# Row maxima of an attention sweep: float16 parts made by GpSimd, turned in four quadrants, copied by ScalarE and sent on-chip into the query stacks

## The chip, the core and the metric

The kernel runs on one core of a Trainium2 chip. A core has a matrix engine (TensorE, "PE" in the profile, its weight loads "PEld"), a vector engine (VectorE, "DVE"), an activation engine (ScalarE, "ACT"), a general engine (GpSimd, "POOL") and a queue engine that here issues all transfers (SyncE, "SP"). Each works through its own instructions in order; semaphores hold an instruction until what it needs is there. TensorE writes into PSUM, eight banks of 128 x 512 float32; the other data is in SBUF.

The metric is the device time of one execution in microseconds (us). The kernel before takes 1451.92 us, the median of 3 runs (1451.56 to 1452.12).

## What is computed

One transformer layer with parallel branches, on 2048 tokens of width 512, 32 heads of 16:

```python
xn = _layernorm(x, axis=-1)
qkv = (xn @ wqkv) ...                                   # 32 heads, head width 16
scores = einsum("bhqd,bhkd->bhqk", q, k) * (Dh ** -0.5)
p = softmax(scores, axis=-1)
o = einsum("bhqk,bhkd->bhqd", p, v) ... @ wo
h = gelu(xn @ w1 + b1)                                  # width 1792
return x + o + (h @ w2 + b2)
```

The softmax takes the maximum of each row of scores off before the exponential. That maximum, for each head and each query, is what the change is about.

## The kernel before

**Two passes over the scores.** The 32 heads are taken in 8 groups of four, the 2048 queries in 4 blocks of 512; a *block* t of the sweep is one group with one query block, so there are 32. Each block has 16 *units*. In unit u TensorE makes four kinds of products:

- **S**: scores of 128 queries against 512 keys, one product for each of the four heads (in the profile `pS<-kst,qst`). VectorE reduces each to one maximum for each query (`mt<-pS`, line 366): four reductions of 128 x 512 in each unit. This is the first pass, and only its maxima are kept.
- **E**: 19 units later (`LEAD`), the same scores again, turned over: 128 keys against 512 queries (`pT<-qst,kst`). ScalarE takes the exponential (`pe<-pT`, line 414).
- **V**: one or two units after that, the products of the exponentials with the values, in float32 (`pV<-pe,vv`), summed over the block's 16 units in one bank.
- **D**: dense products that fill the rest (projections, the two layers of the MLP, the output projection; `pD`), three or four for each half unit, as the table entries `FAST`, `MEAN` and `SLOW` say.

A unit has two halves. In the second one, which the change touches, TensorE's program reads E (head 2), S (head 3), S (head 2), E (head 3), then V, then D. All these products use 64 of the array's 128 rows and are cut into four column groups of 32, so that one product of the upper and one of the lower row half run beside each other; in the order of the program an E of one half stands beside an S of the other.

**Banks.** S products take turns in banks 0 to 2, E products in 3 to 5, D has bank 6, V bank 7. A product waits until its bank's last reader is done: S for the reduction three S products earlier, E for the exponential three E products earlier.

**The maxima.** The Q and K *stacks* (`qst`, `kst`) hold the operands of S and E: each head has 64 rows, of which 48 hold float16 parts of q or k. Rows 62 and 63 hold, in the K stack, the constant 1024, and in the Q stack, minus the query's maximum over 1024, as the sum of two float16 numbers. So the E product already has the maximum taken off; the S product leaves these two rows out. How the maxima come into the rows, for each block, is what changes:

1. at the end of the block's unit 15 (`s_end`), VectorE reduces the block's 64 maxima for each partition to 16 and negates them (`mneg<-mt`, line 382);
2. in the next unit (unit 0 of the next block's S pass), after the first half's products, TensorE turns them over by two float32 products with an identity (`ident,mneg`, line 390; the profile shows two passes for each), into a T or an S bank: S where a dense group has just begun;
3. VectorE reads the result twice and makes the float16 part and its rest (`mhl`, lines 393 and 394);
4. SyncE sends both to a scratch tensor in HBM with two transfers (`m_d<-mhl`, line 397), waits until they are there, and brings them into the stacks' rows with four (`qst<-m_d`, line 348).

The first E product of the block stands at the start of unit 3, that is 2 1/2 units after step 2. VectorE's next work behind step 1 are the four S reductions of unit 0; step 3 stands between its second and third.

**Order of the work.** Outside the first 90 us, nothing is planned at run time or by a scheduler: the program is written unit by unit (`unit`), each engine runs it in that order, and queues (`later`, `pooled`, `run_lane`) only decide in which unit an instruction is written. GpSimd's work is given out at the end of each unit with a budget of `POOL_NS` = 2500 ns. The first part is laid out by a list planner (`Plan`), with an estimated duration for each step; it holds the maxima of block 0.

Of the kernel before, what the change touches and what calls it, by code (L numbers as in the profile page):

```python
# [18 lines left out]
P = 128  # L19
# [15 lines left out]
POOL_NS = 2500  # L35
TAIL = 5
# [11 lines left out]
MROW = 1024.0  # L48
MROWS = struct.unpack("f", struct.pack("ee", MROW, MROW))[0]
# [5 lines left out]
def layer_kernel(ctx: ExitStack, tc: tile.TileContext, x, wqkv, wo, w1, b1, w2, b2, out):  # L55
# [19 lines left out]
    m_d = dram.tile([NG * NQB, 16, 2, P], F16, name="m_d")  # L75
# [21 lines left out]
    mnegs = [const.tile([P, 32], F32, name=f"mneg{i}") for i in range(2)]  # L97
    for m in mnegs:
        nc.gpsimd.memset(m, 0.0)
# [244 lines left out]
    def m_rows(t, h):  # L344
        g, qb = divmod(t, NQB)
        p, a = divmod(h, 2)
        dst = qst[g % 2][qb][64 * a + 62:64 * a + 64, p].rearrange("r (t q) -> r t q", q=P)
        nc.sync.dma_start(dst, m_d[t, 4 * h:4 * h + 4].rearrange("t r q -> r t q"))

    def s_mm(u, n, s):  # L350
# [7 lines left out]
        tiled(None, s, qs[qb][r, p, qt * P:(qt + 1) * P], ks[kb][r, p, :], True, True)  # L358
# [16 lines left out]
    def s_end(u):  # L375
# [4 lines left out]
        g, qb = divmod(t, NQB)  # L380
        mneg = mnegs[t % 2]
        nc.vector.tensor_reduce(mneg[:, :16], mt_of[t].rearrange("p h t k -> p (h t) k"), axis=AX.X, op=ALU.max, negate=True)
        given("dve", 220)

        def store():
# [3 lines left out]
            for a in range(2):  # L389
                nc.tensor.matmul(pt[32 * a:32 * a + 32, :64], mneg[64 * a:64 * a + 64, :],  # L390
                                 ident[64 * a:64 * a + 64, 64 * a:64 * a + 64], start=True, stop=True)
            mhl = work.tile([64, 2, 64], F16, name="mhl", bufs=2)
            nc.vector.tensor_scalar_mul(mhl[:, 0], pt[:64, :64], 1.0 / MROW)
            nc.vector.scalar_tensor_tensor(mhl[:, 1], pt[:64, :64], 1.0 / MROW, mhl[:, 0], op0=ALU.mult, op1=ALU.subtract)
            given("dve", 300)
# [96 lines left out]
    def last_one(osb):  # L492

        idle(3)
        on = work.tile([P, 4, 4, DH], F32, name="on")
# [1022 lines left out]
```

## Time and profile before

| | |
|---|---|
| median of 3 runs | 1451.92 us |
| the profiled execution | 1450.86 us, its span 1449.1 us |
| granted TensorE clock | 0.996 |
| busy: PE, DVE, ACT, POOL | 1432.0, 1353.8, 1255.9, 663.8 us |
| first and last `mneg` reduction of the sweep (31 of them) | 130.6 and 1384.7 us |

The span runs from the first to the last instruction. A matmul's end is modelled, so TensorE's busy time says less than when each product starts. A view of waits puts an engine's idle time down to what ended it; where a row says "issue", nothing that the profile shows ended it.

### The profile page before, as it was taken

The page shows a single profiled execution, that of the slowest core. Times are in us where ns is not written, and L with a number is a line of the kernel's source. Part 1 is how long each engine was busy: PE and PEld are TensorE (multiplying, and loading weights), DVE is VectorE, ACT ScalarE, POOL GpSimd, SP SyncE. Part 2 cuts the span into 40 slices and gives each one's busy share as a digit, 9 for nine tenths or more (in the row PEclk, how much of TensorE's full clock was granted, in tenths as well). Part 3 has the DMA queues.
Part 4 walks back from the last instruction along what each step waited for, and adds up shares of the span by engine and source line. Part 5 has one row for each costly group of instructions (what it writes and reads, how often), then busy time and mean ns, then how long its engine had stood idle before and what let it go on. Part 6 is the DMA issues. An engine that isn't in the chain of part 4 may idle for free.

```text
span 1449.1 us, 88687 instructions
## 1 busy us (share of the span) xinstructions
PE 1432.0 (99%) x40184; PEld 964.6 (67%) x40184; DVE 1353.8 (93%) x2304; ACT 1255.9 (87%) x2367; POOL 663.8 (46%) x673
## 2 busy tenths in 40 slices
PE   8999999999999999999999999999999999999998
PEld 4447767776666767667677766676766767666565
DVE  7989999999999999999999999999999999999933
ACT  5868888888999888899988899998889999888885
POOL 3201857664878401388831138882115787121100
PEclk9999999999999999999999999999999999999999
DMA  7731565455224210221112111121112110111423
GB/s 218 226 122 40 163 202 182 150 181 153 86 64 131 67 34 27 62 70 42 45 44 89 30 37 46 55 74 45 44 39 85 48 38 23 56 55 47 137 65 119
DMA packets 112627, 124.86 MB, mean 86 GB/s; under 512 B 22908, under 2 KB 84220, under 8 KB 112248
## 3 DMA queue, kind: packets, MB, share of 16 engines
q1 hardware_dynamic: 112248, 119.18, 26.8%
q8 instruction: 314, 5.14, 1.5%
q14 instruction: 65, 0.53, 0.1%
HBM read 81.66 MB, written 37.34 MB: 82 GB/s over the span
## 4 chain that ended last, share of the span: by engine, by line
PE 87%; DVE 8%; DMA 2%; ACT 1%; issue 1%; SPq 0%; DVEq 0%; ACTq 0%
PE pD L169 26%; PE pV L169 25%; PE pT L169 17%; PE pS L169 16%; DVE mt L366 7%; PE pT L1015 2%; DMA wq<-in_A_wqkv_dram 1%; PE pD L1015 1%; DMA m_d<-mhl 0%; ACT xs L968 0%; DVE xt L998 0%; ACT pe L414 0%; DMA qst<-m_d 0%; DVE ac L1393 0%; ACT wqk_h L904 0%
## 5 line engine op out<-in xcount | busy, mean ns | idle before, releaser
L366 DVE TENSOR_REDUCE mt<-pS 128x1 f32<-128x512 f32 x2029 | 1277.4, 682 | 34.8 <-PE pS L169 7.8
L414 ACT ACTIVATE pe<-pT 128x512 f32<-128x512 f32 x2048 | 1106.9, 599 | 150.2 <-PE pT L169 65.0
L169 PE MATMUL pV<-pe,vv 64*32 64x512 f32 x8192 | 1087.8, 591 | 0.3 <-issue 0.2
L169 PE MATMUL pT<-qst,kst 64*32 64x512 f16 x8192 | 710.4, 378 | 1.9 <-issue 1.2
L169 PE MATMUL pS<-kst,qst 62*32 62x512 f16 x8116 | 627.0, 378 | 2.6 <-DVE mt L366 2.0
L169 PEld LDWEIGHTS <-qst 62*32 62x32 f16 x8192 | 309.3, 90 | 196.7 <-issue 50.9
L169 PE MATMUL pD<-xb,wc 64*32 64x512 f16 x5376 | 363.9, 375 | 0.0
L169 PE MATMUL pD<-w_s,g 64*32 64x512 f16 x5376 | 361.8, 375 | 0.0
L169 PEld LDWEIGHTS <-kst 64*32 64x32 f16 x8192 | 280.5, 91 | 96.0 <-issue 24.2
L169 PEld LDWEIGHTS pV<-pe,vv 64*32 64x32 f32 x8192 | 245.3, 105 | 13.6 <-PE pV L169 4.2
L169 PEld LDWEIGHTS <-wc 64*32 64x32 f16 x5376 | 160.7, 91 | 44.5 <-issue 0.4
L169 PEld LDWEIGHTS <-g 64*32 64x32 f16 x5376 | 163.5, 91 | 39.2 <-issue 0.5
L169 PE MATMUL pD<-xt,wqk_h 64*32 64x512 f16 x2400 | 159.3, 376 | 0.7 <-issue 0.7
L1360 POOL TENSOR_TENSOR xa<-xa,yt 128x512 f32<-128x512 f32 x16 | 20.5, 1281 | 222.8 <-ACT yt L1358 222.8
L471 POOL TENSOR_TENSOR osb<-osb,rb 128x512 f32<-128x512 f32 x31 | 39.9, 1286 | 159.2 <-DMA rb<-den_d 132.8
L1312 POOL TENSOR_TENSOR t<-hh 128x512 f32<-128x512 f32 x56 | 58.2, 1040 | 77.0 <-ACT hh L1335 75.9
L169 PEld LDWEIGHTS <-wqk_h 64*32 64x32 f16 x2400 | 74.0, 92 | 19.9 <-issue 2.0
L1314 POOL TENSOR_TENSOR t<-t,hh 128x512 f32<-128x512 f32 x56 | 71.8, 1282 | 4.7
L1307 POOL TENSOR_TENSOR t<-t,hh 128x512 f32<-128x512 f32 x56 | 71.7, 1280 | 4.7
L1309 POOL TENSOR_TENSOR g<-t,g 128x512 f16<-128x512 f32 x56 | 65.2, 1164 | 4.7
L1306 POOL TENSOR_SCALAR t<-t,gs 128x512 f32<-128x512 f32 x56 | 38.8, 694 | 54.8 <-ACT t L1301 54.8
L169 PE MATMUL pD<-wo_s,oc 64*32 64x512 f16 x816 | 54.7, 376 | 0.0
(165 smaller groups left out, 895.1 us busy)
## 6 DMA issues: line engine op xcount, KB each, us to landing
wc<-w_d SPq DMA_DIRECT2D x56, 256.0 KB
qk_d<-stg SPq DMA_DIRECT2D x32, 256.0 KB
rb<-den_d SPq DMA_DIRECT2D x124, 64.0 KB
wch<-in_B_w_dram SPq DMA_DIRECT2D x14, 512.0 KB
wch<-in_B_w_dram SPq DMA_DIRECT2D x28, 256.0 KB
w_d<-wsp SPq DMA_DIRECT2D x28, 256.0 KB
kst<-qk_d SPq DMA_DIRECT2D x64, 96.0 KB
qst<-qk_d SPq DMA_DIRECT2D x64, 96.0 KB
```

The source lines that it names most:

```text
L169: p = nc.tensor.matmul(*args, **kw)
L366: nc.vector.reduce_max(mt_of[t][:, n, qt, kb:kb + 1], s, axis=AX.X)
L414: nc.scalar.activation(pe, st, AF.Exp, scale=scale_of[g // 2])
L471: pooled((1280, lambda: nc.gpsimd.tensor_tensor(osb, osb, rb, op=ALU.mult)), (620, lambda: nc.gpsimd.tensor_scalar(ot[:, 0], osb, 1.0, 0.0 ...
L1015: nc.tensor.matmul(tl[key], lhs, rhs, start=c + n == 0, stop=(c, n) == (NC - 1, 2))
L1306: pooled((690, lambda: nc.gpsimd.tensor_scalar(t1, t1, 1.0, gs[:, 1:2], op0=ALU.add, op1=ALU.mult)), (1280, lambda: nc.gpsimd.tensor_tenso ...
L1307: (1280, lambda: nc.gpsimd.tensor_tensor(t1, t1, hh, op=ALU.mult)),
L1309: (1160, lambda: nc.gpsimd.tensor_tensor(g[:, 1, f, :], t1, g[:, 0, f, :], op=ALU.subtract)),
L1312: pooled((1040, lambda: nc.gpsimd.tensor_tensor(t1, hh, hh, op=ALU.mult)), (620, lambda: nc.gpsimd.tensor_scalar(t1, t1, 1.0, 1.0 / GELU_A ...
L1314: (1280, lambda: nc.gpsimd.tensor_tensor(t1, t1, hh, op=ALU.mult)),
L1360: add = lambda: nc.gpsimd.tensor_tensor(xa, xa, yt, op=ALU.add)
```

## The change

After the change the steps for each block are these:

1. VectorE reduces to 16 maxima, without the sign (`mx<-mt`).
2. GpSimd divides by 1024 and makes the float16 part and its rest, three instructions of 128 x 16 elements, in the tile `mparts` (lines 363 to 365 of the changed kernel).
3. TensorE turns them with a negated float16 identity: 16 products of 64 rows, 32 columns, 64 moving columns (`m_turn`, line 373), each in one of four quadrants of 64 x 32 of the array, four times. They stand in the second half of unit 0, behind its second S product and ahead of its last E.
4. ScalarE copies 128 x 256 elements to float16 (`m_copy`, line 378).
5. SyncE issues four transfers from SBUF to SBUF, one for each head, straight into the stacks' rows (line 354). Nothing goes to HBM.

For the rows of a head to come out in one piece, the S products take their queries in another order: a tile of 128 queries is now two runs of 64 that lie 256 apart (`s_mm`). GpSimd's budget depends on the unit: 800 ns at the end of unit 14, 3100 ns at the end of units 15, 0 and 1 (`POOL_AT`), 2500 ns elsewhere, which makes 40,100 ns for each block in place of 40,000. Block 0 takes the same steps in the planner's part.

```diff
-    mnegs = [const.tile([P, 32], F32, name=f"mneg{i}") for i in range(2)]
+    nident = const.tile([P, P // 2], F16, name="nident")
+    for a in range(2):
+        nc.gpsimd.tensor_scalar(nident[64 * a:64 * a + 64], ident[64 * a:64 * a + 64, 64 * a:64 * a + 64], -1.0, 0.0,
+                                op0=ALU.mult, op1=ALU.add)
+    mparts = [const.tile([P, 64], F16, name=f"mparts{i}") for i in range(2)]
...
-        room[0] = min(room[0], 0) + POOL_NS
+        room[0] = min(room[0], 0) + (POOL_AT.get(pos[0] % 16, POOL_NS) if pos[0] < NU else POOL_NS)
...
+    def m_rows(t, turned, p, a):
         g, qb = divmod(t, NQB)
+        row = 64 * a + 62
+        nc.sync.dma_start(qst[g % 2][qb][row:row + 2, p, :], turned[2 * p + a:P:32])
+
+    def m_parts(t):
+        mx = work.tile([P, 4, 4], F32, name="mx", bufs=1)
+        parts = mparts[t % 2]
+        hi, lo = (parts[:, 16 * j:16 * j + 16].rearrange("p (t n) -> p n t", n=4) for j in range(2))
+        flat = mx.rearrange("p n t -> p (n t)")
+        return (lambda: nc.vector.tensor_reduce(flat, mt_of[t].rearrange("p h t k -> p (h t) k"), axis=AX.X, op=ALU.max),
+                lambda: nc.gpsimd.tensor_scalar(flat, flat, 1.0 / MROW, 0.0, op0=ALU.mult, op1=ALU.add),
+                lambda: nc.gpsimd.tensor_scalar(hi, mx, 1.0, 0.0, op0=ALU.mult, op1=ALU.add),
+                lambda: nc.gpsimd.tensor_tensor(lo, mx, hi, op=ALU.subtract)), parts
+
+    def m_turn(pt, parts):
+        for qt in range(4):
+            for j in range(2):
+                for s in range(2):
+                    row, c = 32 * (2 * j + s), 16 * j + 4 * qt
+                    nc.tensor.matmul(pt[row:row + 32, 64 * qt:64 * qt + 64], parts[64 * s:64 * s + 64, c:c + 32],
+                                     nident[64 * s:64 * s + 64], start=True, stop=True)
+
+    def m_copy(pt):
+        turned = work.tile([P, QB // 2], F16, name="mturned", bufs=2)
+        nc.scalar.activation(turned, pt[:, :QB // 2], AF.Copy)
...
-        tiled(None, s, qs[qb][r, p, qt * P:(qt + 1) * P], ks[kb][r, p, :], True, True)
+        for j in range(0, P, 32):
+            c = QB // 2 * (j // 64) + 64 * qt + j % 64
+            product(None, s[j:j + 32], qs[qb][r, p, c:c + 32], ks[kb][r, p, :], start=True, stop=True)
...
-            for a in range(2):
-                nc.tensor.matmul(pt[32 * a:32 * a + 32, :64], mneg[64 * a:64 * a + 64, :],
-                                 ident[64 * a:64 * a + 64, 64 * a:64 * a + 64], start=True, stop=True)
-            mhl = work.tile([64, 2, 64], F16, name="mhl", bufs=2)
-            nc.vector.tensor_scalar_mul(mhl[:, 0], pt[:64, :64], 1.0 / MROW)
-            nc.vector.scalar_tensor_tensor(mhl[:, 1], pt[:64, :64], 1.0 / MROW, mhl[:, 0], op0=ALU.mult, op1=ALU.subtract)
-            for a in range(2):
-                nc.sync.dma_start(m_d[t, :, :, 64 * a:64 * a + 64], mhl[32 * a:32 * a + 16])
-            for h in range(4):
-                m_rows(t, h)
+            m_turn(pt, parts)
+            turned = m_copy(pt)
+            for p, a in FIRST:
+                m_rows(t, turned, p, a)
...
+            for i, (kind, b) in enumerate(((1, 1), (0, 0), (0, 1), (1, 0)) if a == 0 else ((1, 2), (0, 3), (0, 2), (1, 3))):
+                if a == 1 and i == 3 and u % 16 == 0 and u // 16 - 1 in stores:
+                    stores.pop(u // 16 - 1)()
...
-            if a == 0 and u % 16 == 0 and u // 16 - 1 in stores:
-                stores.pop(u // 16 - 1)()
```

What this moves shows best in the order of each engine's instructions. On VectorE, at the end of a block in the MLP (the rows are runs of equal instructions: `mt<-pS` are the S reductions, `dn` another step of the softmax), before:

```order
L366 TENSOR_REDUCE mt<-pS 128x1 [waits PE_49] x20
L382 TENSOR_REDUCE mneg_100<-mt 128x16 [waits DVE_49]
L366 TENSOR_REDUCE mt<-pS 128x1 [waits PE_49] x2
L393 TENSOR_SCALAR mhl<-pT 64x64 [waits DMAHW0_49,PE_49]
L394 SCALAR_TENSOR_TENSOR mhl<-pT,mhl 64x64 [waits DVE_49]
L366 TENSOR_REDUCE mt<-pS 128x1 [waits PE_49] x42
```

and now:

```order
L485 RECIPROCAL dn<-dn 64x32 [waits DMAHW7_49,DMAHW4_49]
L400 TENSOR_REDUCE mt<-pS 128x1 [waits PE_49] x20
L362 TENSOR_REDUCE mx<-mt 128x16 [waits DVE_49,Pool_49]
L400 TENSOR_REDUCE mt<-pS 128x1 [waits PE_49] x44
L485 RECIPROCAL dn<-dn 64x32 [waits DMAHW3_49,DMAHW0_49]
```

The two `mhl` instructions between the second and the third reduction of the next unit are gone from VectorE; the reductions follow each other.

On TensorE, in unit 0 behind block 8 (an identity product is `ident` or `nident`; `pS` is an S, `pT` an E product, or the bank of the turn), before:

```order
L169 MATMUL pD<-xb,wc 32x512
L390 MATMUL pT<-ident,mneg_100 32x64 [waits DVE_49,Activation_49]
L390 MATMUL pT<-ident,mneg_100 32x64
L169 LDWEIGHTS kst_3_86
L169 MATMUL pT<-qst_3_94,kst_3_86 32x512 [waits Activation_49]
```

and now, at the start of the turn:

```order
L176 LDWEIGHTS qst_1_87
L176 MATMUL pS<-kst_0_78,qst_1_87 32x512
L373 LDWEIGHTS mparts_102 [waits Pool_49]
L373 MATMUL pT<-nident,mparts_102 32x64 [waits Activation_49]
L373 LDWEIGHTS mparts_102
L373 MATMUL pT<-nident,mparts_102 32x64
```

The turn stood behind the dense products of the unit's first half; it now stands three products later, behind the second half's last S product, and its first weight load waits for GpSimd. Behind its 32 instructions come the unit's last E, the V and the D products.

On GpSimd, at the end of block 8, in the MLP (`t` and `g` are steps of its GELU, `osb` and `ot` the softmax's last steps), before:

```order
L1309 TENSOR_TENSOR g<-t_12832,g 128x512 [waits Pool_49]
L1312 TENSOR_TENSOR t_13482<-hh 128x512 [waits Activation_49,Pool_49]
L1313 TENSOR_SCALAR t_13482<-t_13482 128x512 [waits Pool_49]
L1314 TENSOR_TENSOR t_13482<-t_13482,hh 128x512 [waits Pool_49]
L471 TENSOR_TENSOR osb<-osb,rb 128x512 [waits DMAHW4_49,DMAHW5_49,DMAHW3_49,DMAHW6_49,DMAHW2_49,DMAHW1_49]
```

and now:

```order
L1327 TENSOR_TENSOR g<-t_12954,g 128x512 [waits Pool_49]
L363 TENSOR_SCALAR mx<-mx 128x16 [waits DVE_49]
L364 TENSOR_SCALAR mparts_102<-mx 128x4x4 [waits PE_49,Pool_49]
L365 TENSOR_TENSOR mparts_102<-mx,mparts_102 128x4x4 [waits PE_49,Pool_49]
L1330 TENSOR_TENSOR t_13608<-hh 128x512 [waits Activation_49]
L1331 TENSOR_SCALAR t_13608<-t_13608 128x512 [waits Pool_49]
```

The three small instructions stand ahead of work that was behind the same `g` step before, and the first of them waits for VectorE's maxima, with that work queued behind it.

More of the change, by code (lines that the diff above doesn't have):

```diff
@@ L35 @@
 POOL_NS = 2500
+POOL_AT = {15: 800, 0: 3100, 1: 3100, 2: 3100}
 TAIL = 5
@@ L48 @@
 MROW = 1024.0
+FIRST = (0, 1), (0, 0), (1, 0), (1, 1)
 MROWS = struct.unpack("f", struct.pack("ee", MROW, MROW))[0]
@@ L379, in s_end @@
             return
-        g, qb = divmod(t, NQB)
-        mneg = mnegs[t % 2]
-        nc.vector.tensor_reduce(mneg[:, :16], mt_of[t].rearrange("p h t k -> p (h t) k"), axis=AX.X, op=ALU.max, negate=True)
+        steps, parts = m_parts(t)
+        for step in steps:
+            step()
         given("dve", 220)
@@ L1128, in layer_kernel @@
             score(u)
[L1130 to L1135 removed]
+        mkey, m_of = ("S", "m", 0), []
+        m_steps, m0 = m_parts(0)
+        a = add("DVE", 220, m_steps[0], m_last)
+        for step in m_steps[1:]:
+            a = add("POOL", 220, step, [a])
         def turn_m():
             tl[mkey] = sb_tile(mkey)
[L1139 to L1141 removed]
+            m_turn(tl[mkey], m0)
         a = add("PE", 300, turn_m, [a], take=[mkey])
[L1144 to L1152 removed]
+        a = add("ACT", 340, lambda: m_of.append(m_copy(tl[mkey])), [a], free=[mkey])
+        for k in FIRST:
+            add("SP", 270, lambda k=k: m_rows(0, m_of[0], *k), [a], size=4, tail=E_TAIL)
         for t in range(NV):
```

32 lines of the change are left out of this document (5 added, 27 removed).

## The prediction, made before the changed kernel ran

> **What bounds the kernel now.** First the page's busy times, then its chain of waits.
>
> ```profile
> PE 1432.0 (99%) x40184; PEld 964.6 (67%) x40184; DVE 1353.8 (93%) x2304; ACT 1255.9 (87%) x2367; POOL 663.8 (46%) x673
> PE 87%; DVE 8%; DMA 2%; ACT 1%; issue 1%; SPq 0%; DVEq 0%; ACTq 0%
> ```
>
> TensorE is the bound, and VectorE stands right behind it: only 8% of the chain runs through it, but with 93% busy it cannot fall back. How closely the two run is read from three blocks in the view by windows, cut from one maxima reduction to the next (columns: window, its length, then for PE, PEld, DVE, ACT and POOL busy time and instructions, clock, DMA share, GB/s), with its sum over 31 blocks.
>
> ```profile
> 551.20:592.00 40.80, 40.80 (x1228) 28.98 (x1220) 40.44 (x68) 35.78 (x68) 6.50 (x6) 1.00 0.10 28
> 922.50:964.10 41.60, 41.40 (x1228) 28.09 (x1220) 40.83 (x68) 39.03 (x76) 33.88 (x36) 1.00 0.28 84
> 1006.20:1048.20 42.00, 42.00 (x1284) 29.50 (x1273) 41.28 (x68) 35.57 (x67) 5.59 (x5) 1.00 0.14 40
> sum 1299.50, PE 1294.10 PEld 892.51 DVE 1267.48 ACT 1153.21 POOL 638.88; mean PE 41.75 PEld 28.79 DVE 40.89 ACT 37.20 POOL 20.61
> ```
>
> A block with full dense work takes 42.0 us, 2.62 for each of its 16 units; one with less takes 40.8, and VectorE is busy in 40.44 of them. So a microsecond taken from VectorE is worth a microsecond only where TensorE is not already at its own pace, and a microsecond added to TensorE's program is nearly always paid. I therefore follow both engines through the first two units after the maxima; all times from here count from the start of the maxima reduction. The timeline of VectorE, in a block of middling dense work:
>
> ```profile
> 757.75 0.22 DVE L382 TENSOR_REDUCE mneg<-mt 128x16 f32<-128x64 f32 x1
> 757.88 1.28 DVE L366 TENSOR_REDUCE mt<-pS 128x1 f32<-128x512 f32 x2
> 759.08 0.21 DVE L393 TENSOR_SCALAR mhl<-pT 64x64 f16<-64x64 f32 x1
> 759.32 0.22 DVE L394 SCALAR_TENSOR_TENSOR mhl<-pT,mhl 64x64 f16<-64x64 f32 x1
> 759.46 6.09 DVE L366 TENSOR_REDUCE mt<-pS 128x1 f32<-128x512 f32 x10
> ```
>
> Ten reductions in 6.09 us are one every 0.60. Without the two `mhl` the third reduction would start where the first of them does, at 759.08: they cost VectorE 0.38 us (759.46 less 759.08), not the 0.43 of their durations. TensorE in the same stretch (weight loads in the second row):
>
> ```profile
> 757.40 0.65 PE L169 MATMUL pV<-pe,vv 64*32 64x512 f32 x4
> 758.12 0.17 PEld L390 LDWEIGHTS pT<-ident,mneg 64*32 64x32 f32 x2
> 758.45 0.22 PE L390 MATMUL pT<-ident,mneg 64*32 64x64 f32 x1
> 758.50 0.51 PE L169 MATMUL pS<-kst,qst 62*32 62x512 f16 x5
> 758.72 0.39 PE L169 MATMUL pT<-qst,kst 64*32 64x512 f16 x2
> 758.85 0.60 PE L169 MATMUL pV<-pe,vv 64*32 64x512 f32 x3
> 760.18 0.40 PE L169 MATMUL pS<-kst,qst 62*32 62x512 f16 x4
> 760.40 0.61 PE L169 MATMUL pV<-pe,vv 64*32 64x512 f32 x4
> ```
>
> The V products of unit 0's first half start at 757.40, those of its second half at 758.85, those of unit 1's first half at 760.40, 2.65 after the maxima. The last step is long because the S at 760.18 waits for a bank whose reduction, pushed back by `mhl`, ends near 760.13 (759.46 plus one 0.67). The same 2.65 stands in a full block (1006.22 to 1008.87) and in one of light work (345.98 to 348.64):
>
> ```profile
> 1006.22 0.22 DVE L382 TENSOR_REDUCE mneg<-mt 128x16 f32<-128x64 f32 x1
> 1008.87 0.59 PE L169 MATMUL pV<-pe,vv 64*32 64x512 f32 x1
> 345.98 0.22 DVE L382 TENSOR_REDUCE mneg<-mt 128x16 f32<-128x64 f32 x1
> 348.64 0.61 PE L169 MATMUL pV<-pe,vv 64*32 64x512 f32 x4
> ```
>
> So at this point VectorE sets TensorE's pace, whatever the dense work. Six blocks differ, those whose turn takes an S bank; the turn then holds up the S products themselves, and the same V products come 3.01 after the maxima:
>
> ```profile
> 386.82 0.22 DVE L382 TENSOR_REDUCE mneg<-mt 128x16 f32<-128x64 f32 x1
> 389.83 0.60 PE L169 MATMUL pV<-pe,vv 64*32 64x512 f32 x3
> ```
>
> **The change part by part.** *VectorE* loses `mhl`, 0.38 us for each block. If nothing else came in, the V products could start 0.38 earlier, at 2.27; over 31 blocks that is 11.8 us, the most this part can bring.
>
> *GpSimd.* No instruction of 128 x 16 elements stands in the trace; the nearest rows give it.
>
> ```profile
> L1240 POOL TENSOR_TENSOR gs<-facv,fac 128x1 f32<-128x1 f32 x1 | 0.2, 189 | 19.2 <-DVE fac L138 19.2
> L1218 POOL TENSOR_SCALAR wsp<-wch 128x1024 f16<-128x1024 f32 x14 | 14.6, 1045 | 1.1
> L626 POOL TENSOR_SCALAR stg<-pf 128x512 f16<-128x512 f32 x25 | 15.4, 618 | 43.3 <-DMA qk_d<-stg 18.3 <-ACT pf L625 17.0 <-ACT pe L414 8.0
> L1313 POOL TENSOR_SCALAR t<-t 128x512 f32<-128x512 f32 x56 | 34.6, 618 | 4.9
> ```
>
> From 512 to 1024 elements the time grows by 427 ns, 0.83 for each, so 16 take 0.19 + 0.01 = 0.20 us, and a dependent instruction starts 0.09 after the one before (4.9 us over 56). Maxima end at 0.22; three times 0.29 later the parts are there, at 1.09. GpSimd must be free by then: by the order, the instruction ahead of the three at block 8 is the one at 422.70 here, which ends 4.5 us before the maxima reduction at 428.33:
>
> ```profile
> 422.70 1.17 POOL L1309 TENSOR_TENSOR g<-t,g 128x512 f16<-128x512 f32 x1
> 428.33 0.22 DVE L382 TENSOR_REDUCE mneg<-mt 128x16 f32<-128x64 f32 x1
> ```
>
> What is behind them waits up to that long; at 20.61 us busy of a mean block of 41.9 (34 in the fullest) GpSimd can afford it, and I cost it at nothing; without this slack ScalarE would wait for GELU steps.
>
> *TensorE* is where it is decided. By the order the turn stands behind unit 0's last S product, and E, V, D queue behind it. That S waits for the first reduction of the unit, which ends near 0.82 (757.88 plus 0.68), so it starts near 0.87, as the row at 758.50 (five S products, ending at 759.01) shows. The turn's weights wait for the parts: 1.09 plus what a wait costs TensorE, 0.15 by the rows above (maxima end at 757.97, the first weight load follows at 758.12) or 0.05 if the load came late for another reason; so 1.14 to 1.24. Then 16 products in four rounds of four quadrants. The old turn's four passes took from 758.12 to 758.45, 0.33 with weights; a float16 round streams 64 columns where 512 take about 0.215 (one S at 758.50, the next behind it at 758.72), 0.03, and can't be faster than its weight reload. I take 0.05 for a round and 0.2 to 0.25 in all: the four quadrants run beside each other, as the four groups of every other product here do. The last E then starts at 1.34 to 1.49, V 0.13 behind it (758.72 to 758.85) at 1.47 to 1.62, against 1.10 before. Half a unit later, 1.31 in a full block, unit 1's V starts at 2.78 to 2.93 in place of 2.65: **+0.13 to +0.28 for each block**, +0.2 taken. VectorE's gain is then used up: its next S comes late by as much as it is early. In blocks of light dense work the half unit is shorter, 1.2 (four reductions of 0.60 make a unit of 2.4), and it is +0.1. In the six with an S bank the turn moves behind the second reduction (near 1.42 by 757.88 + 1.28), so V comes at about 1.8 and 3.1, +0.1.
>
> Sum of TensorE: 20 blocks x 0.2, five light ones x 0.1, six x 0.1: +5.1 us. The old turn's time in the first half needs no term, since the 2.65 did not depend on it.
>
> *ScalarE* gets 31 copies of 256 elements, at most the 0.6 us of an exponential of 512. It is busy 37.20 of 41.9 us, 39.03 in the fullest block shown; the exponential behind the copy comes later, but nothing waits for it within two units. Nothing, up to 0.1 for each block if that cover is gone.
>
> *Transfers.* The path had two trips, one to HBM and one back, and SyncE stood between them.
>
> ```profile
> SPq L348 <- DMA m_d<-mhl: 51.8, 38, 3.0
> PEld L169 <- DMA qst<-m_d: 2.8, 5, 0.9
> ```
>
> TensorE waited for the rows five times, 2.8 us in all. One trip in place of two brings the rows in about 3 us earlier, while the copy ends about 0.8 later than `mhl` did; these waits go: -2.0 taken, 0 to -2.8.
>
> In all +5.1 - 2.0 = **+3.1 us**: 1450.86 becomes about 1454. The profiled execution lies 1.1 us under the median, so on the runs' scale **1455.0**, 0.2% slower, at the edge of the 0.2% (2.9 us) that a measurement here can tell.
>
> **The rivals.** *Faster: the parts come in time.* If GpSimd and the semaphores need 0.2 less, the turn starts with the last S at 0.87, takes 0.2, and unit 1's V starts at 1.07 + 0.13 + 1.31 = 2.51: 25 blocks x -0.14, less 2.0 for the transfers, is -5.5, or 1446.4. For it: VectorE is 93% busy and its `mhl` sits where TensorE waits. Against it: three dependent instructions at 0.29.
>
> *Break-even.* The parts come at the early end and the transfers bring their full 2.8: 25 x 0.08 - 2.8, about 1451.
>
> *Clearly slower: the 16 products run one after the other.* The quadrants alternate between the two row halves and write one bank. If that makes them wait for each other, 16 take 16 x 0.03 (their streams) to 16 x 0.055 (the old passes stood at 758.29 to 758.45, three steps in 0.16), 0.5 to 0.9 in place of 0.2: +0.3 to +0.7 for each of 31 blocks, 1464 to 1477. It decides from about 0.03 us for each product on. Against it: four column groups of every other product start within 0.02 of each other. The Trainium skill ("TensorEngine Tiling (Array Packing)", Instruction Overhead) says that a matmul of up to about 60 columns costs the same as one of a single column, about 60 cycles; at its 2.4 GHz that is 25 ns, and 16 in a row would be 0.4, an estimate that gives 1461. The rows here show only how groups of 512 columns overlap, so the trace does not decide between them.
>
> *GpSimd falls behind*: in the twelve blocks with 34 us of its work, a wait of 5 leaves under 2 spare; a microsecond lost in each makes 1467.
>
> *It does not do what it says*: the one trip is as slow as two, and TensorE goes on waiting for rows; 1457.
>
> **How the numbers follow.** Forecast 0.45 (half of it within 0.2%), faster 0.23, break-even 0.10, one after the other 0.14, GpSimd late 0.05, no shorter trip 0.03. So faster 0.23, same 0.32, slower 0.45. The forecast's own range is 1451 to 1459; for eight in ten it reaches to 1444, into the faster case (its bound, all of 11.8 and 2.8 gained, lies at 1437), and to 1464, where the serial case begins.
>
> **What would show it.** In the changed profile's timeline: the three GpSimd instructions at about 200 ns, the last ending 0.9 us after the maxima; the first weight load of the turn 0.05 to 0.15 behind it; the 16 products within 0.25; unit 1's V products 2.8 to 2.9 after the maxima (2.5 if the faster case holds, 3.1 and more for the serial one). VectorE's busy time falls by about 13 us, 31 x 0.43, without the span following. No wait of a weight load for the rows' transfer should be left. It is wrong if V stands at 2.65 or less in most blocks, or if the span changes through blocks' other units.

## The result and the profile after

The changed kernel takes 1458.97 us (median of 6 runs, 1456.87 to 1461.80), the kernel before 1451.74 in the same session (6 runs, 1449.73 to 1452.18). The ratio is 1.0054, 95% interval 1.0038 to 1.0070: some 7.8 us slower. The forecast was 1455.0, its range 1444 to 1464, so the sign was right and the size less than half of it. First the changed kernel's busy times and its chain of waits:

```profile
PE 1440.9 (99%) x40568; PEld 973.1 (67%) x40568; DVE 1353.0 (93%) x2240; ACT 1265.4 (87%) x2399; POOL 684.4 (47%) x771
PE 91%; DVE 6%; ACT 1%; DMA 1%; issue 0%; DVEq 0%; SPq 0%; POOL 0%; ACTq 0%
```

TensorE holds 91% of the chain in place of 87%. VectorE was to lose 13 us of busy time and lost 0.8; rows that explain a part of it come below, with the start. What TensorE waits for in the changed kernel (the view of waits; the sum in us, how often, the longest):

```profile
PEld L373 <- POOL mparts L365: 6.4, 27, 0.6
```

The weight loads of the turn wait for GpSimd's parts in 27 of 32 blocks, 6.4 us. No row on the stacks' rows is left. One block with full dense work in the timeline (the block that stood at 1006.22 in the kernel before; rows of other work left out):

```profile
1016.91 0.22 DVE L362 TENSOR_REDUCE mx<-mt 128x16 f32<-128x64 f32 x1
1017.22 0.20 POOL L363 TENSOR_SCALAR mx<-mx 128x16 f32<-128x16 f32 x1 [8.06 <-DVE mx L362]
1017.50 0.23 POOL L364 TENSOR_SCALAR mparts<-mx 128x16 f16<-128x16 f32 x1
1017.81 0.23 POOL L365 TENSOR_TENSOR mparts<-mx,mparts 128x16 f16<-128x16 f32 x1
...
1018.10 0.15 PEld L373 LDWEIGHTS <-mparts 64*32 64x32 f16 x12 [0.21 <-POOL mparts L365]
1018.10 0.24 PE L373 MATMUL pT<-nident,mparts 64*32 64x64 f16 x8
...
1018.18 0.61 PE L176 MATMUL pV<-pe,vv 64*32 64x512 f32 x1
...
1019.68 0.65 PE L176 MATMUL pV<-pe,vv 64*32 64x512 f32 x4
```

From the start of the maxima: parts at 1.13 (1017.81 plus 0.23), first weight load at 1.19, unit 0's second V at 1.27, unit 1's first V at 2.77 (2.65 before).

To see where the 7.8 us lie, I cut both executions at the E products, by the start of each unit's first one: the start (up to the first E product of all); the "turn windows" (in each of the 31 blocks that have a turn after the start, the four units from the one with the turn on); all other units; and the end (from the start of the third last unit on).

| us | start | 31 turn windows | other units | end | span |
|---|---|---|---|---|---|
| before | 93.18 | 329.4 | 1004.3 | 22.2 | 1449.1 |
| changed, first profile | 99.77 | 332.5 | 1005.6 | 22.1 | 1460.0 |
| changed, second profile (run `again`) | 98.36 | 332.5 | 1001.7 | 22.1 | 1454.7 |

The windows give +3.1 in both profiles of the change, to a tenth of a microsecond. The larger share, +5.2 to +6.6, lies in the start, where I had put nothing. The other units differ by 4 us between two executions of the same kernel, so nothing of 1 or 2 us is read from them.

### The profile page after: what moved, and what is told of

Same layout as the page of the kernel before. It is cut to its first block, busy times and chain, and to the rows that moved or that the text cites. A ratio compares the mean times of both kernels' runs of the same rounds, so it can differ in the third digit from the quotient of the medians.

```text
span 1460.0 us, 89513 instructions
## 1 busy us (share of the span) xinstructions
PE 1440.9 (99%) x40568; PEld 973.1 (67%) x40568; DVE 1353.0 (93%) x2240; ACT 1265.4 (87%) x2399; POOL 684.4 (47%) x771
## 4 chain that ended last, share of the span: by engine, by line
PE 91%; DVE 6%; ACT 1%; DMA 1%; issue 0%; DVEq 0%; SPq 0%; POOL 0%; ACTq 0%
PE pD L176 28%; PE pV L176 26%; PE pT L176 18%; PE pS L176 17%; DVE mt L400 4%; PE pT L1042 1%; PE pD L1042 0%; DVE bs L980 0%; DMA wq<-in_A_wqkv_dram 0%; DVE sd L982 0%; DMA xs<-in_A_x_dram 0%; DVE xt L1025 0%; PE pT L373 0%; DVE ac L1411 0%; DVE wvh L1125 0%
## 5 line engine op out<-in xcount | busy, mean ns | idle before, releaser
L176 PEld LDWEIGHTS <-kst 64*32 64x32 f16 x8192 | 282.7, 91 | 93.4 <-issue 22.6
L363 POOL TENSOR_SCALAR mx<-mx 128x16 f32<-128x16 f32 x32 | 6.5, 204 | 304.6 <-DVE mx L362 300.6
```

The lines of the kernel that those rows point to most:

```text
L176: p = nc.tensor.matmul(*args, **kw)
L363: lambda: nc.gpsimd.tensor_scalar(flat, flat, 1.0 / MROW, 0.0, op0=ALU.mult, op1=ALU.add),
```

## The experiments

All times are medians; the ratio is to the kernel before on the same chip in the same session (its medians: 1449.65 to 1450.77). "First E" and "windows" are the first two columns of the table above.

| run | us | ratio (95%) | first E | windows |
|---|---|---|---|---|
| again | 1457.36 | 1.0053 (1.0041 to 1.0065) | 98.36 | 332.5 |
| old_start | 1453.60 | 1.0022 (1.0013 to 1.0031) | 93.89 | 332.4 |
| new_start | 1457.18 | 1.0048 (1.0036 to 1.0060) | 98.01 | 329.8 |
| late_setup | 1457.68 | 1.0043 (1.0030 to 1.0056) | 97.66 | 332.5 |
| turn_half | 1456.59 | 1.0044 (1.0031 to 1.0057) | 99.88 | 330.7 |
| hi_only | 1452.82 | 1.0015 (1.0006 to 1.0024) | 97.18 | 328.9 |
| twice | 1461.07 | 1.0081 (1.0060 to 1.0103) | 97.91 | 336.9 |
| dve_parts | 1482.06 | 1.0208 (1.0188 to 1.0227) | 97.87 | 360.3 |
| relief | 1446.35 | 0.9973 (0.9963 to 0.9982) | 93.07 | 326.0 |
| round_trip | 1458.54 | 1.0048 (1.0030 to 1.0066) | 97.42 | 332.3 |
| split | 1453.85 | 1.0023 (1.0013 to 1.0033) | 93.70 | 332.1 |
| split_near | 1609.12 | 1.1100 (1.1072 to 1.1129) | 93.71 | 467.6 |

### The start

`again` is the changed kernel once more.

> The changed kernel once more, for a second profile of its start. Theory A (the loss has two places: the start of the kernel, whose order the change rearranged, and the turn in each block): 1457 to 1462, and the first E product at 97 to 100 us (93.2 before). Theory B (only the blocks cost; that the first E product came 6.6 us later in the one profile was chance): 1457 to 1462 too, but the first E product anywhere between 93 and 100, as in any other kernel here.

`old_start` takes only block 0's maxima back to the old way; a helper copies the old `m_rows` under another name, and block 0's S products take their queries in the old order.

```
-        m_steps, m0 = m_parts(0)
-        a = add("DVE", 220, m_steps[0], m_last)
-        for step in m_steps[1:]: a = add("POOL", 220, step, [a])
-        ...  (m_turn, m_copy, four m_rows)
+        a = add("DVE", 220, maxima, m_last)
+        ...  (mneg0, two passes, mhl by VectorE, two writes to m_d, four reads)
```

> The changed kernel, but with the maxima of block 0 alone by the old way (mneg, two passes, mhl, m_d), so that the start has the old order. Theory A: the first E product is back at 93 to 94 us, and the time falls to the old one plus the blocks' share of 3.1, 1454 to 1456. Theory B: 1457 to 1460, the start makes no difference that holds.

`new_start` is the kernel before with the opposite edit: block 0's maxima alone by the new way.

> The kernel before, but with the maxima of block 0 alone by the new way, so that only the start has the new order. Theory A: the first E product at 97 to 100 us, 1454 to 1459, and unit 1's V products at 2.65 as before. Theory B: 1451 to 1453.

The first E products of five kernels, in the timeline of TensorE (before, `old_start`, changed, `again`, `new_start`, one row of each):

```profile
93.18 0.39 PE L169 MATMUL pT<-qst,kst 64*32 64x512 f16 x4
```

```profile
93.89 0.39 PE L179 MATMUL pT<-qst,kst 64*32 64x512 f16 x4
```

```profile
99.77 0.39 PE L176 MATMUL pT<-qst,kst 64*32 64x512 f16 x4
```

```profile
98.36 0.39 PE L176 MATMUL pT<-qst,kst 64*32 64x512 f16 x4
```

```profile
98.01 0.39 PE L181 MATMUL pT<-qst,kst 64*32 64x512 f16 x4
```

Theory A holds. The five kernels that start in the old order (before, `old_start`, `relief`, `split`, `split_near`) come to the first E between 93.07 and 93.89; the seven profiles with the changed kernel's start order between 97.42 and 99.88, on average 4.9 later (`hi_only` and `dve_parts` have orders of their own: 97.18 and 97.87). `old_start` brings the time to +3.2 us, which is the windows' share (1.9 to 4.5 by its interval). `new_start` has the windows of before and yet takes +7.0; its profiled run has only +4.8 in the start, so some 2 us of its time are not accounted for by its profile, and its runs spread over 4.7 us. The two halves add to 10.2 where the whole is 7.7; the intervals are 1.3 to 1.7 us to either side, and what is left between them stays open.

Why is the start longer? The edit stands at its end, where block 0's maxima are turned at about 91 us. But the start is ordered by a planner, and with other steps in that last chain it put its work into another order from about 32 us on. `old_start` has the order of the kernel before again, apart from GpSimd's setup, and `new_start` that of the changed kernel. The place where it costs, as far as the rows show it, on ScalarE, TensorE and VectorE of the kernel before:

```profile
35.25 0.82 PE L1015 MATMUL pD<-xt,wqk_h 128*128 128x512 f16 x3
39.59 0.57 ACT L1027 ACTIVATE stg<-pD 128x512 f16<-128x512 f32 x1
50.04 0.18 DVE L961 RECIPROCAL sd<-sd 128x4 f32<-128x4 f32 x1
```

and of the changed kernel (in brackets: idle before it, and what ended it):

```profile
45.22 0.82 PE L1042 MATMUL pD<-xt,wqk_h 128*128 128x512 f16 x3
46.12 0.60 ACT L1054 ACTIVATE stg<-pD 128x512 f16<-128x512 f32 x1 [2.61 <-issue]
54.20 0.18 DVE L988 RECIPROCAL sd<-sd 128x4 f32<-128x4 f32 x1
64.22 0.66 PE L1012 MATMUL pT<-ident,xs 128*128 128x128 f32 x4 [1.70 <-ACT vv L1139]
64.71 3.79 PE L1042 MATMUL pT<-xt,wqk_h 128*128 128x512 f16 x9
```

The query products of the second quarter (the 12 on `xt,wqk_h` into `pD`) now end at 46.0 in place of 36.1, and ScalarE, which has to copy them out at that point of its queue, stands idle for 2.61 us with the rest of the normalization behind it. The last quarter's reciprocal comes 4.2 later, and TensorE then waits 1.70 for ScalarE, 0.72 in the kernel before. All seven profiles with this order show the two idle times, 2.60 to 2.61 on ScalarE and 1.70 to 1.71 on TensorE; the five with the old order have 0.72 to 0.73 on TensorE and not the one on ScalarE. That the order costs the 4.9 us is shown by the runs; that it does so by way of these products is read from the rows, and no run moves them alone. In two of the seven profiles, this one among them, the granted clock falls behind that wait, and the nine products take 3.79 in place of 2.11 in `again` (view by windows, columns as in the prediction, changed and `again`):

```profile
64.00:70.00 6.00, 5.78 (x34) 2.31 (x35) 1.12 (x2) 4.51 (x10) 1.31 (x2) 0.72 0.79 211
```

```profile
64.00:70.00 6.00, 5.51 (x46) 2.24 (x46) 2.53 (x5) 5.12 (x10) 1.60 (x2) 1.00 0.66 193
```

The two with the lower clock are those with the first E at 99.8 and 99.9; the other five lie between 97.4 and 98.4. What makes the clock fall in some executions and not in others, after the same idle time, no run here shows.

`late_setup` tests a second suspect in the start: VectorE's two small instructions on `sd`.

```
-    for a in range(2): nc.gpsimd.tensor_scalar(nident[...], ident[...], -1.0, 0.0, ...)
-    for m in mparts: nc.gpsimd.memset(m.bitcast(F32), 0.0)
-            add("POOL", 720, lambda k=k: clear(1, [k]), tail=-9000)
+            add("POOL", 720, lambda k=k: (clear(1, [k]), setup() if k == 3 else None), tail=-9000)
```

> The changed kernel with the setting up of nident and the parts' buffers moved behind GpSimd's sixteen memsets of the stacks (order of the start otherwise the same). Theory P (the four setup instructions push the memsets 0.6 us later, and VectorE's two small instructions on sd wait for the last memset): sd waits 0.6 or less as before, its reciprocal comes near 10.3 in place of 11.25, the first E product 0.5 to 1.0 us earlier, 1456 to 1457. Rival: sd waits to the last memset all the same; reciprocal at 10.6 to 10.8, the rest as in the changed kernel. Either way the rearranged order keeps its 4 us and more: the first E product not below 96.

Both instructions as the timeline has them, changed and `late_setup`:

```profile
7.46 3.12 DVE L982 TENSOR_SCALAR sd<-mv 128x4 f32<-128x4 f32 x1
7.53 3.05 DVE L983 TENSOR_SCALAR sd<-mv 128x4 f32<-128x4 f32 x1
```

```profile
8.09 0.35 DVE L981 TENSOR_SCALAR sd<-mv 128x4 f32<-128x4 f32 x1
8.17 0.28 DVE L982 TENSOR_SCALAR sd<-mv 128x4 f32<-128x4 f32 x1
```

In the changed kernel they last 3.1 us, until 10.58, where GpSimd's last memset ends (10.03 plus 0.52); with the setup behind the memsets, 0.3, although three memsets still follow. `turn_half`, which has the setup ahead and the same start of 8.09, shows 2.49. So the wait hangs on GpSimd's queue and goes when the setup is moved; why it ends with one memset in one case and goes on over six in the other, no run here shows. It is worth little: the reciprocal behind it comes at 10.68 in place of 11.24, the first E at 97.66 lies among the others, the time is the same within its interval, and `old_start`, whose two instructions last 3.3, comes to its first E at 93.89. Theory P had the wait right; reciprocal, first E and time are the rival's. Together with the same two instructions near 50 us (1.16 and 1.11, in a stretch in which GpSimd is busy) these waits add 7.4 us to the two rows of `sd` below (changed, then before). The two instructions overlap, so 4.4 of it count in VectorE's busy time:

```profile
L982 DVE TENSOR_SCALAR sd<-mv 128x4 f32<-128x4 f32 x4 | 4.6, 1155 | 0.1
L983 DVE TENSOR_SCALAR sd<-mv 128x4 f32<-128x4 f32 x4 | 4.5, 1116 | 0.0
```

```profile
L956 DVE TENSOR_SCALAR sd<-mv 128x4 f32<-128x4 f32 x4 | 1.0, 257 | 0.0
L955 DVE TENSOR_SCALAR sd<-mv 128x4 f32<-128x4 f32 x4 | 0.7, 172 | 0.1
```

### The turn: wait or products

`turn_half` moves the turn half a unit later, where the parts have long been there.

```
-                if a == 1 and i == 3 and u % 16 == 0 and u // 16 - 1 in stores:
+                if a == 0 and i == 0 and u % 16 == 1 and u // 16 - 1 in stores:
```

> The changed kernel with the turn half a unit later (ahead of unit 1's first E), when GpSimd's parts have been there for about 0.8 us. Theory C (TensorE pays for waiting for the parts): the first weight load of the turn waits for nothing, unit 0's second V comes near 1.06 in place of 1.27, unit 1's first V at 2.5 to 2.6 in place of 2.78, and the time falls by 3 to 6 us against the changed kernel. Theory D (TensorE pays for the 16 products wherever they stand, one step of about 0.21 us): V comes late by the same 0.2 half a unit further on, and the time is that of the changed kernel within 1.5 us.

`hi_only` shortens GpSimd's work to one instruction.

```
-                lambda: nc.gpsimd.tensor_scalar(flat, flat, 1.0 / MROW, 0.0, op0=ALU.mult, op1=ALU.add),
-                lambda: nc.gpsimd.tensor_scalar(hi, mx, 1.0, 0.0, op0=ALU.mult, op1=ALU.add),
-                lambda: nc.gpsimd.tensor_tensor(lo, mx, hi, op=ALU.subtract)), parts
+                lambda: nc.gpsimd.tensor_scalar(hi, mx, 1.0 / MROW, 0.0, op0=ALU.mult, op1=ALU.add)), parts
```

> The changed kernel with one GpSimd instruction in place of three: the high part alone, scaled and rounded; the low part is left out (its columns stay zero). All 16 products stay. The parts are then there about 0.55 us after the maxima in place of 1.14. Theory C2 (the wait for the parts costs 0.18 a block): unit 0's second V at 1.07 to 1.10 in place of 1.27, unit 1's first V at 2.60 to 2.70 in place of 2.78, the first four units of the blocks 2 to 4 us less in sum (332.5 in the changed kernel), 1453 to 1456. Theory D (only the products cost, and the wait is made up for): V stays at 2.78 and the time at 1457.

`twice` doubles the products.

```
             m_turn(pt, parts)
+            m_turn(pt, parts)
```

> The changed kernel with the 16 products done twice into the same bank. Theory D: what the turn costs is the stream of its products, 0.2 to 0.29 us for 16 wherever nothing runs beside them, so unit 1's first V goes from 2.78 to 2.98 to 3.07 and the time rises by 6 to 9 us, 1463 to 1466. Rival (the quadrants run beside each other and beside E, since their starts lie within 0.11 us): V within 0.05 of 2.78, 1457 to 1459.

The same full block in `hi_only` (maxima, part, first weight loads, unit 0's and unit 1's V):

```profile
1009.35 0.22 DVE L362 TENSOR_REDUCE mx<-mt 128x16 f32<-128x64 f32 x1
1009.73 0.23 POOL L363 TENSOR_SCALAR mparts<-mx 128x16 f16<-128x16 f32 x1 [8.13 <-DVE mx L362]
...
1010.26 0.30 PEld L371 LDWEIGHTS <-mparts 64*32 64x32 f16 x12
...
1010.53 0.61 PE L176 MATMUL pV<-pe,vv 64*32 64x512 f32 x1
...
1012.00 0.62 PE L176 MATMUL pV<-pe,vv 64*32 64x512 f32 x4
```

The part is there at 0.61, and the turn starts at 0.91, behind the last S, without a wait. V follows at 1.18 and 2.65: 0.12 earlier than in the changed kernel at unit 1. Over the windows that is 3.6 us (332.5 to 328.9), all of the +3.1 and a little more; the time falls by 5.5 us, of which about 1 is its start. The six blocks whose turn takes an S bank gain nothing: there the first product waits for the bank until 1.47 in both kernels. So the wait for the three GpSimd instructions, which starts the turn 0.28 later, is what the turn lost in this change. `hi_only` is no version to keep, since it leaves the low part out.

`turn_half` gains half of that, 1.8 us. It takes the wait away, but the products pay elsewhere:

```profile
1015.58 0.22 DVE L362 TENSOR_REDUCE mx<-mt 128x16 f32<-128x64 f32 x1
...
1017.54 0.47 PE L373 MATMUL pT<-nident,mparts 64*32 64x64 f16 x16
...
1018.28 0.62 PE L176 MATMUL pV<-pe,vv 64*32 64x512 f32 x4
```

Unit 0's V comes at 1.10, as expected from the wait, yet unit 1's V at 2.70 and not at 2.5: in front of unit 1's E the starts of the 16 products are spread over 0.28 us, 0.11 in the changed kernel, the E behind them starts only after the last, and the half unit takes 1.60, 1.50 in the changed kernel. Theory C overrated, theory D underrated it; the time (-0.8 against `again`, inside the intervals) does not tell.

`twice` prices the products, in the same block:

```profile
1013.05 0.22 DVE L362 TENSOR_REDUCE mx<-mt 128x16 f32<-128x64 f32 x1
...
1014.50 0.66 PE L176 MATMUL pV<-pe,vv 64*32 64x512 f32 x4
...
1015.98 0.63 PE L176 MATMUL pV<-pe,vv 64*32 64x512 f32 x4
```

V stands at 1.45 and 2.93, so 16 more cost 0.15 to 0.18 here; over the windows it is 4.4 us, 0.14 a block, and 4.0 in the time (1.0081 less 1.0053; the intervals are 1.7 and 3.1 us to either side). The forecast had taken 0.2 to 0.25. They are neither free nor one after the other at the price of a separate matmul. The Trainium skill ("TensorEngine Tiling (Array Packing)", Instruction Overhead) gives a short matmul about 60 cycles of its own, from which the prediction's estimate of 0.4 for 16 came; the run does not bear out that these 60 cycles add up for products that go round the four quadrants.

`dve_parts` lets VectorE make the parts, in two instructions.

```
-                lambda: nc.gpsimd.tensor_scalar(...), lambda: nc.gpsimd.tensor_scalar(...), lambda: nc.gpsimd.tensor_tensor(...)
+                lambda: nc.vector.tensor_scalar_mul(hi, mx, 1.0 / MROW),
+                lambda: nc.vector.scalar_tensor_tensor(lo, mx, 1.0 / MROW, hi, op0=ALU.mult, op1=ALU.subtract)), parts
```

> The changed kernel with the parts made by VectorE in two instructions (block 0's too, which gives the start a third order). Theory C2 (the wait for GpSimd is what the turn costs): the parts stand at 0.55 to 0.65 in place of 1.14, unit 0's second V at 1.17, but VectorE's reductions start 0.35 to 0.4 later, so unit 1's first V at 2.65 to 2.80; the first four units of the blocks 329 to 331 in sum (332.5 changed, 328.9 with the high part alone). Rival (VectorE's 0.38 weighs as much as GpSimd's wait): 332 to 335. The time hangs on the start too: 1453 to 1458.

Neither: 1482.06, windows of 360.3. The two instructions take 0.19 and 0.20 in a quiet block, but here is one in which GpSimd works (VectorE's rows, then GpSimd's):

```profile
399.46 0.56 DVE L363 TENSOR_SCALAR mparts<-mx 128x16 f16<-128x16 f32 x1
400.05 1.20 DVE L364 SCALAR_TENSOR_TENSOR mparts<-mx,mparts 128x16 f16<-128x16 f32 x1
```

```profile
398.81 1.17 POOL L1326 TENSOR_TENSOR g<-t,g 128x512 f16<-128x512 f32 x1
399.94 1.26 POOL L497 TENSOR_TENSOR osb<-osb,rb 128x512 f32<-128x512 f32 x1
```

The first ends at 400.02 with GpSimd's instruction (399.98), the second at 401.25 with the next one (401.20). VectorE waits in the middle of its queue for GpSimd, with the reductions behind it, and TensorE waits 22.6 us for those (26 times in its view of waits, 2.0 the longest). `mhl` of the kernel before did not suffer this: its two instructions read a bank and took 207 and 217 ns on average over 24 blocks.

```profile
L394 DVE SCALAR_TENSOR_TENSOR mhl<-pT,mhl 64x64 f16<-64x64 f32 x24 | 5.2, 217 | 0.8
L393 DVE TENSOR_SCALAR mhl<-pT 64x64 f16<-64x64 f32 x24 | 5.0, 207 | 0.0
```

The Trainium skill ("SBUF — State Buffer", SBUF: two separate sides) says that VectorE in some modes, or with two inputs in SBUF, and GpSimd share a pair of ports that one of them holds for a whole instruction. The rows at 399.46 and 400.05 agree, to within 0.05 us. The `sd` rows at 7.46 agree that GpSimd blocks VectorE, but there the wait went on over six memsets, not one.

### VectorE's share, and the rows

`relief` is the kernel before with `mhl` off VectorE: ScalarE makes the high part, and the low part is left out.

```
-            nc.vector.tensor_scalar_mul(mhl[:, 0], pt[:64, :64], 1.0 / MROW)
-            nc.vector.scalar_tensor_tensor(mhl[:, 1], pt[:64, :64], 1.0 / MROW, mhl[:, 0], op0=ALU.mult, op1=ALU.subtract)
+            nc.scalar.activation(mhl[:, 0], pt[:64, :64], AF.Copy, scale=1.0 / MROW)
```

> The kernel before with mhl taken from VectorE alone: ScalarE makes the high part, the low part is left out (zero), all else as before. The prediction's reading (VectorE sets the 2.65, pushed back by mhl): unit 1's first V at 2.27 to 2.45, the first four units of the blocks 6 to 11 us less in sum (329.4 before), 1439 to 1444. Rival (TensorE's own products already stand there: old turn 0.33 and half a unit 1.31): V at 2.55 or later, 1 to 3 us less, 1447 to 1449.

A full block and one with light dense work:

```profile
1003.75 0.22 DVE L385 TENSOR_REDUCE mneg<-mt 128x16 f32<-128x64 f32 x1
1006.36 0.68 PE L172 MATMUL pV<-pe,vv 64*32 64x512 f32 x4
...
552.26 0.22 DVE L385 TENSOR_REDUCE mneg<-mt 128x16 f32<-128x64 f32 x1
554.74 0.59 PE L172 MATMUL pV<-pe,vv 64*32 64x512 f32 x1
```

Unit 1's V comes at 2.61 in the full block, 0.04 earlier than before; at 2.48 in the light one, 0.17 earlier, and at 2.28 to 2.40 in some others. The windows give 3.5 us of the 11.8 that I had called the most, the time 3.9. And 1.5 of the 3.5 stand in the two blocks in which the kernel before waited longest for the rows (599.60 and 765.47), a wait that is gone in `relief`; so VectorE's share is nearer to 2. In full blocks V stands at 2.6 even without `mhl`, and the profile shows no wait of TensorE of 0.15 us or more on the way there, so its own products are the likely bound; VectorE set the 2.65 only in the light ones.

`round_trip` takes the changed kernel's rows through HBM again.

```
-            for p, a in FIRST: m_rows(t, turned, p, a)
+            for n in range(4): nc.sync.dma_start(m_d[t, n], turned[n:P:32])
+            for p, a in FIRST: far_rows(t, p, a)      (one read from m_d[t, 2 * p + a] each)
```

> The changed kernel with its rows taken through HBM again: four writes of the turned rows, four reads into the stacks. The prediction's term for the transfers (2.0 us, 0 to 2.8): weight loads wait for the rows again, 1 to 3 us in sum, 1458 to 1460. Rival (the rows come early enough either way, the waits of before came from the queue's other work): no wait, 1457.

No weight load waits for the rows, the windows are those of the changed kernel (332.3), and the time is the same within the intervals. The rival was right: a trip through HBM has no price here, at least when each read needs only one of the writes. The waits of the kernel before (2.8 us) went with the change, but not because one trip took the place of two; `relief`, which has two as well, shows none either. What the five waits have in common is a late read: in the kernel before each of a block's four reads needs both writes, the fourth is issued between 4.9 and 7.0 us after the maxima, and in the five blocks at 6.5 or later. In `round_trip` it is never later than 6.2.

`split` and `split_near` were to keep `relief`'s gain with the low part in place. Both make both parts from a copy that ScalarE takes out of the bank; GpSimd's budgets are those of the change, and a small tile of the softmax's last steps (`on`) shares a buffer.

```
+            nc.scalar.activation(mcp, pt[:64, :64], AF.Copy, scale=1.0 / MROW)
+            nc.gpsimd.tensor_scalar(mhl[:, 0], mcp, 1.0, 0.0, op0=ALU.mult, op1=ALU.add)
+            nc.gpsimd.tensor_tensor(mhl[:, 1], mcp, mhl[:, 0], op=ALU.subtract)
             (split: two writes to m_d, four reads; split_near: 16 transfers mhl[...] -> qst[...])
```

> The kernel before, whole in its results, with mhl taken from VectorE: ScalarE copies the turned maxima out of the bank, scaled, GpSimd splits the copy into high and low part (two instructions), the rows go by HBM as before; GpSimd's step budgets as in the change. By the run without the low part (1446.35): first four units 325.5 to 327 in sum, no weight load waits for the rows, first E product at 93 to 94, 1445 to 1448. Rival (GpSimd's two instructions stand behind its other work and the rows come late): weight loads wait for the rows 3 to 10 us in sum, 1449 to 1456.

> As the run before it, but the rows go straight into the stacks, by 16 transfers of four short pieces each in place of two writes and four reads. If a trip through HBM has no price here: the same time within 1.5 us. If rows were late there: the waits go, and it is faster by as much. Rival: 16 transfers hold up SyncE's queue, and what stands behind them (the weights of the dense work, the next stacks) comes late: 1 to 4 us slower.

What the weight loads wait for in `split`, then what weight loads and products wait for in `split_near` (the views of waits), and last the row of SyncE's issues for one block of `split_near` (timeline; start, length):

```profile
PEld L170 <- DMA qst<-m_d: 9.9, 10, 2.2
```

```profile
PEld L170 <- DMA qst<-mhl: 42.5, 26, 3.4
PE pT L170 <- DMA qst<-mhl: 104.0, 87, 2.9
```

```profile
557.12 10.07 SPq L357 DMA_DIRECT2D qst<-mhl  x16
```

`split`'s rival decided: where GpSimd is busy its two instructions come late, and ten blocks wait for their rows; where it is not, the windows are `relief`'s (10.74, 10.38 and 10.20 in the same blocks). `split_near` is slower by 11%: SyncE needs 10.07 us to issue 16 transfers, 0.6 each, the E products wait for them, and every block's window is 3.6 to 6.4 us longer than in the kernel before. Its rival had the place right and the size far too small. So no complete version here beats the kernel before; `relief` does by 0.27%, with the low part missing.

## Point by point

**What bounds the kernel.** TensorE, as said. "So at this point VectorE sets TensorE's pace, whatever the dense work" was wrong for full blocks: `relief` moves V there by 0.04 of the 0.38 that VectorE gains, in light blocks by 0.17 to 0.37.

**GpSimd's parts.** 0.20, 0.23 and 0.23 us, the last ending 1.13 after the maxima (1.09 forecast). Right. The parts stand at 1.13 or 1.14 in all 32 blocks, the busy ones among them, so GpSimd was free in time. That the work behind them costs nothing is not shown by itself; nothing in the windows or the waits points to a price.

**TensorE waits for them.** Right, but for the six blocks that wait for an S bank, and `hi_only` shows it by taking the wait away: 3.6 us over the windows. The first weight load comes 0.06 behind the parts, at the short end of 0.05 to 0.15.

**The 16 products** take 0.14 to 0.18 a block by `twice`, 0.2 to 0.25 forecast. They start within 0.11, and E and V start while they still stream: V stands at 1.27, not at 1.47 to 1.62. The path was misread on the side of the kernel before, too: its 1.10 for V came from a lighter block. In the full block (maxima at 1006.22) unit 0's second V stood at 1.21, and the half unit behind it took 1.44, not 1.31:

```profile
1007.43 0.66 PE L169 MATMUL pV<-pe,vv 64*32 64x512 f32 x4
```

So the change puts this V 0.06 later, and the half unit behind it takes 1.50, another 0.06 to 0.07: unit 1's V comes at 2.77, where 2.78 to 2.93 was forecast. That the end of the path fits is in part luck, two errors in its middle against each other.

**ScalarE's copies** were to cost nothing, up to 0.1 a block. `hi_only` keeps them all, and in the full block its V of unit 1 stands at 2.65, as in the kernel before; they have no price that shows.

**The windows.** The eight blocks with V at 1.21 to 1.22 before +0.17 to +0.38 (0.2 forecast), six others with V at 1.20 to 1.35 only -0.07 to +0.09; most light ones +0.12 to +0.18 (0.1 forecast), two 0.04 earlier; the six with an S bank +0.09 to +0.16 (0.1), the last block +0.35. In all +3.06, of which -0.84 in the two blocks in which the kernel before waited longest for rows (599.60 and 765.47), so +3.9 for the turn in the other 29 against +5.1 for all.

**Transfers.** The waits went, and all five stood in the windows. The two longest show: these two windows are 0.84 shorter, where light blocks like them are 0.17 longer, so some 1.2 us came by it, an estimate from these windows; -2.0 was forecast. The reason given fell with `round_trip`.

**VectorE's busy time** was to fall by 13 us. `mhl` did go, but its instructions overlap the reductions, so it made up only 8.8 of the busy time; 4.4 came back as waiting for GpSimd in the `sd` instructions of the start, and the reductions' own rows grew by 2.8.

**Where the number failed.** Forecast +3.1, measured +7.2 to +7.8. The step that failed is the sum, "In all +5.1 - 2.0 = +3.1 us": all its terms are blocks, and the start had none. I had read the edit of the start as moving a chain at its end and not compared how the planner ordered the rest. The start costs 4.9 us on average over the profiles; `old_start` takes it back, and then the time is +3.2, the forecast almost to the digit. So close a fit is luck: the turn cost about 1 us less than its term and the transfers brought about 1 us less than theirs. Not tested alone are the new order of the queries in S and GpSimd's budgets; both act on all units, and the other units differ less from the kernel before than the two profiles of the change do from each other.

## What to carry over

Where a planner sets the order, an edit of its last steps can move work 60 us ahead of them: compare the order of every engine from the top, not only around the edit, and price the difference as a term of its own. When an in-order engine queues behind a chain of short instructions of another engine, cut the chain before moving the wait: one GpSimd instruction in place of three (with the low part left out) took 3.6 us out of the windows, the same turn half a unit later 1.8, since the products then paid elsewhere. Count a path of many small transfers by what its issuing engine needs for each, here 0.6 us, before counting the trip.

## What the runs showed of the hardware

- A VectorE instruction of 128 x 16 from SBUF to SBUF took 0.19 us beside an idle GpSimd and up to 1.26 beside a busy one, ending within 0.05 us of GpSimd's instruction in the block shown; those of 64 x 64 that read a bank took 0.21 to 0.22 in all 32 blocks. At the start two of 128 x 4 lasted 3.1 us over a row of memsets, and 0.35 when the memsets ran 0.7 earlier and the two began 0.6 later.
- 16 float16 products of 64 columns in four quadrants cost 0.14 to 0.18 us more when done a second time.
- SyncE took 0.6 us to issue a transfer of four pieces of 128 bytes, and as long for one of 2 KB from SBUF (2.35 us for four).
- After the same 1.7 us of idle TensorE, the granted clock over the next 6 us was 0.72 in two of seven profiles and 1.00 in five.
